# Attention: the weighted values of every second unit in two halves of 256 queries, and the products of a pair of units in another order

## The chip, the cores and the metric

The kernel runs on one core of a Trainium2 chip. The metric is the device time of one execution in microseconds (us): the median of 3 runs before the change is 1863.93 us (1863.89 to 1864.54). Beside it stands one profiled execution, from which all rows of the profile come; its own time is 1863.55 us.

A core has five engines that work side by side, each with its own queue of instructions in a fixed order: PE (matrix products; the loads of its weights are shown apart, as PEld), DVE (elementwise work and reductions), ACT (activations), POOL and SP (here the issuer of DMAs). They wait for one another by semaphores. PE writes its products to PSUM, which has eight banks of 128 partitions by 512 fp32 values.

## The reference

One transformer block over 2048 rows of 512 values: attention with 32 heads of 16, and then a gated mixer.

```python
h = x + _A_ref(_layernorm(x), A_wqkv, A_wo)
...
qkv = (x @ wqkv).reshape(B, S, 3, H, Dh) ...
scores = jnp.einsum("bhqd,bhkd->bhqk", q, k) * scale
p = _softmax(scores, axis=-1)
o = jnp.einsum("bhqk,bhkd->bhqd", p, v)
return o.transpose(...).reshape(B, S, D) @ wo
...
h2 = h + _B_ref(_layernorm(h), ...)
```

The change lies in the attention, in the scores, their maxima and the weighted values; the mixer behind it is the same code in both kernels.

## The kernel before

**Stages.** A first stage normalizes x and makes q, k and v (up to about 172 us of the span). Then comes the attention loop (to about 1408 us), then the mixer.

**The attention loop.** The 32 heads are taken in 8 groups of 4 (`hg`), the 2048 queries in 4 blocks of 512 (`qb`), the keys in 16 blocks of 128 (`kb`). One `(hg, qb, kb)` is a unit, 512 in all. The loop (L744) takes two units a pass, which is called a pair here: unit A with an even `kb`, unit B with `kb1`. PE, ACT, DVE and SP keep the order in which the code is written (`manual_schedule`), so the lines of the loop are the order of their queues.

**A unit's own work.** `score(hg, qb, kb, p)` (L665) is called for p = 0 and 1. It makes two products `s` (L673), for t = 0 and t = 1: keys by queries, 128 by 512. The operands for t = 0 lie in partitions from 0, those for t = 1 in partitions from 64 (`RG` = 64, `KM` = 50 rows). Then ACT takes the exp of both at once into the tile `pt` (L676). The pool of `s` has two buffers of two banks each. `weigh` (L679) makes the weighted values of a unit: for each of the 4 heads a product of 32 columns of weights (the values of the head, a column of ones for the sum, the rest padding) with `pt`, 512 queries wide (L684). The four write to four bands of 32 partitions of the one bank `pv`, and sum over the 16 key blocks there: `start` at `kb == 0`, `stop` at the last. Each fp32 product is two instructions, so a call is eight. `weigh` of a unit runs behind the scores of the next; `prev` is the unit B of the pair before.

**gather.** When a sum of 16 key blocks is finished (at `kb == 0` of the next), `gather` (L687) copies `pv` to SBUF, half by DVE (L690) and half by ACT (L694), and stores it. A `weigh` with `kb == 0` writes the same bank anew. `invert` (at `kb == 6`, L648) takes the reciprocals of the sums, on DVE.

**The maxima.** Softmax needs the maximum of each row of the scores ahead of the exp. `max_pair(m)` (L207) gives eight steps, one product `m` each (L225: 128 queries by 512 keys), which run in the same pair of units as other scores, but `LEAD` = 11 pairs ahead of them. `four[0]` to `four[3]` are `one(1, e, b)`: t = 1, with a DVE maximum over the row (L230). `one(0, 2)` and `one(0, 3)` are the same for t = 0. For the first half of the keys with t = 0 there are `minus`, whose product ACT takes the Abs of (L235), and `plus`, whose product DVE joins with it (L239). The number that a step is called with is its bank, 0 to 2 (`bank`, L202); a step into a bank waits for the DVE or ACT instruction that read it last. There are steps in the pairs with n from 0 to 488, 245 of them; the last eleven pairs have none. In every eighth pair `last` also joins the maxima of a block of queries (`nm`, L245), POOL splits them in two parts (L90, L93), and `max_rows` (L255) transposes them on DVE (L259) and stores them by eight DMAs as rows of `qst`, where a later `score` reads them.

**The order of a pair before.** On PE, with t in brackets and W for the eight instructions of a `weigh`: s(0) s(1) s(0) s(1) of unit A, `four[0]`(1), `one(0,2)`(0), W of `prev`, `minus`(0), [gather], `four[1]`(1), s(0) s(1) of unit B, `four[2]`(1), s(0) s(1), `four[3]`(1), `plus`(0), W of unit A, [`max_rows`], `one(0,3)`(0).

Of the kernel before, what the change touches and what calls it, by code (L numbers as in the profile page):

```python
# [8 lines left out]
F32 = mybir.dt.float32  # L9
# [3 lines left out]
AF = mybir.ActivationFunctionType  # L13
# [5 lines left out]
P = 128  # L19
# [3 lines left out]
DH = 16  # L23
# [3 lines left out]
NB = S // P  # L27
HB = NB // 2
NQ = S // 512
DB = D // P  # L30
HG = H // 4
# [17 lines left out]
def block_kernel(ctx: ExitStack, tc: tile.TileContext, x, wqkv, wo, w_in, w_sp4, b_sp, w_out, out):  # L49
# [154 lines left out]
            return more[i]()  # L204
        return ps_m.tile([P, 512], F32, name=f"m{i}")

    def max_pair(m):  # L207

        g, i = divmod(m, 8)
        hg, qb = divmod(g, NQ)
        q, k, w = qst[g], kst[hg % 2], uvs[hg % 2]
        if i == 0:
            mx[g] = sm.tile([P, 16, 4], F32, name="mx")
            nc.gpsimd.memset(mx[g][:, :8, 3:], LOW)
        c, p = slice(i % 4 * P, i % 4 * P + P), i // 4
        at = lambda t, e: mx[g][:, t * 8 + i, e:e + 1]  # L220

        def scores(t, keys, b):
            r = slice(RG * t, RG * t + KS)
            acc = bank(b)
            nc.tensor.matmul(acc, q[r, p, c], keys[r, p], start=True, stop=True)  # L225
            return acc

        def one(t, e, b):
            acc = scores(t, k[:, :, 512 * e:512 * e + 512], b)
            nc.vector.reduce_max(at(t, e if t else e - 1), acc, axis=AX.X)  # L230

        def minus(b):
            acc = scores(0, w[:, :, 512:], b)
            ab[0] = sm.tile([P, 512], F32, name="ab")
            nc.scalar.activation(ab[0], acc, AF.Abs)  # L235

        def plus(b):
            acc = scores(0, w[:, :, :512], b)
            nc.vector.tensor_tensor_reduce(ab[0], acc, ab[0], 0.5, LOW, ALU.add, ALU.max, at(0, 0))  # L239

        def last(b):
            one(0, 3, b)
            if i == 7:
                nm = sm.tile([P, 2, 8], F32, name="nm")
                nc.vector.tensor_reduce(nm.rearrange("p t i -> p (t i)"), mx.pop(g), axis=AX.X,  # L245
                                        op=ALU.max, negate=True)
                parts = sm.tile([P, 2, 2, 8], F32R, name="mparts")
                split(parts[:, :, 0], parts[:, :, 1], nm, "pool", "pool")
                turned[0] = (g, parts)

        ab = {}
        four = [lambda b, e=e: one(1, e, b) for e in range(4)]
        return [four[0], lambda b: one(0, 2, b), minus, four[1], four[2], four[3], plus, last]

    def max_rows():  # L255

# [398 lines left out]
    with ExitStack() as at:  # L655
# [6 lines left out]
        ps_s = at.enter_context(tc.tile_pool(name="ps_s", bufs=2, space=PSUM))  # L662
        pv = {}

        def score(hg, qb, kb, p):  # L665

            q, k = qst[hg * NQ + qb], kst[hg % 2]
            turn[0] += len(later)
            pool = later[0] if later and turn[0] % 3 == 2 else ps_s
            s = pool.tile([P, 2, 512], F32, name="s")  # L670
            for t in range(2):
                r = slice(RG * t, RG * t + KM)
                nc.tensor.matmul(s[:, t, :], k[r, p, kb * P:(kb + 1) * P], q[r, p, :],  # L673
                                 start=True, stop=True)
            t = pp.tile([P, 2, 512], F32, name="pt")
            nc.scalar.activation(t, s, AF.Exp, scale=DH ** -0.5)  # L676
            return t

        def weigh(hg, qb, kb, pts):  # L679
            if kb == 0:  # L680
                pv[0] = ps_v.tile([P, 512], F32, name="pv")
            for j in range(4):
                c = (4 * kb + j) * VW
                nc.tensor.matmul(pv[0][32 * j:32 * j + 32, :], vst[hg % 2][:, c:c + 32],  # L684
                                 pts[j % 2][:, j // 2, :], start=kb == 0, stop=kb == NB - 1)

        def gather(hg, qb, pool=sm):  # L687

            o = pp.tile([P, 512], F32, name="o", bufs=1)
            nc.vector.tensor_copy(o[:, :256], pv[0][:, :256])  # L690
            if pool is sm and later:
                nc.vector.tensor_copy(o[:, 256:], pv[0][:, 256:])
            else:
                nc.scalar.activation(o[:, 256:], pv[0][:, 256:], AF.Copy)  # L694
            cols = slice(qb * 512, (qb + 1) * 512)
            sums = pool.tile([P, 16], F32, name="sums")
            for j in range(4):
                h = head(hg, j % 2, j // 2)
                nc.sync.dma_start(o_scr[h * DH:(h + 1) * DH, cols], o[32 * j:32 * j + DH, :])
                nc.sync.dma_start(sums[32 * j:32 * j + 32, :], o[32 * j + DH:32 * j + VW, :])  # L700
            sums_[0] = (hg, cols, sums, pool)
# [18 lines left out]
        def more_h(k):  # L720

            for _ in range(k):
                if not pieces:
                    sb = h_rows[len(hns)]
                    acc = later[0].tile([P, 512], F32, name="h")
                    pieces.extend([sb, acc, h_products(sb, acc)])
                sb, acc, products = pieces
                next(products)
                made[0] += 1
                if made[0] % (3 * DB):  # L730
                    continue
                pieces.clear()
                add_h(sb, acc)
                split_o(h_rows[len(hns) + 1], *("pool", "pool") if hns else [None])
                mv, rs = scale_h(sb)
                hns[sb] = e2.tile([P, D], F32, name="hn", bufs=3)
                nc.vector.tensor_scalar(hns[sb], xrs.pop(sb), mv[:, 0:1], rs,
                                        op0=ALU.subtract, op1=ALU.mult)
# [4 lines left out]
        with tc.manual_schedule(engines={E.PE, E.Activation, E.DVE, E.SP}):  # L743
            for n in range(0, len(units), 2):  # L744
                (hg, qb, kb), (_, _, kb1) = units[n:n + 2]
                if hg + 1 < HG and n % 64 < 24 and n % 4 == 0:
                    load_k(hg + 1, [n % 64 // 4])
                if hg + 1 < HG and n % 64 < 12 and n % 4 == 2:
                    load_uv(hg + 1, [n % 64 // 4])
                if hg + 1 < HG and n % 64 == 30:  # L750
                    load_v(hg + 1)
                if kb == 2 and n // NB + 3 < HG * NQ:
                    load_q(n // NB + 3)
                steps = max_pair(m) if m < 8 * HG * NQ else []
                m += 1
                if not steps and not later:
                    maxima.close()
                    later.append(attn.enter_context(
                        tc.tile_pool(name="ps_l", bufs=1, space=PSUM, side="right")))
                step = lambda b: steps and steps.pop(0)(b)  # L760
                pts = [score(hg, qb, kb, 0), score(hg, qb, kb, 1)]
                step(2)
                step(0)
                if prev is None:

                    pv[0] = ps_v.tile([P, 512], F32, name="pv")
                    for j in range(4):
                        nc.tensor.matmul(pv[0][32 * j:32 * j + 32, :], vst[0][:, :32],
                                         vst[0][:, :512], start=True, stop=True)
                else:  # L770
                    weigh(*prev)
                step(1)
                if kb == 0 and n:
                    gather(*units[n - 1][:2])
                step(2)
                pts1 = [score(hg, qb, kb1, 0)]
                step(0)
                pts1.append(score(hg, qb, kb1, 1))
                step(1)
                step(2)  # L780
                if n >= 490:
                    more_h(2 + (n < 494))
                weigh(hg, qb, kb, pts)
                if turned:
                    max_rows()
                step(1)
                prev = (hg, qb, kb1, pts1)
                if kb == 6 and n > NB:
                    invert()
                if n % 32 == 16 and n < 6 * 32:  # L790
                    load_weights(n // 32)
                if n in (476, 482, 492, 504):
                    load_o(h_rows[(476, 482, 492, 504).index(n)])
                if n == 482:
                    split_o(h_rows[0], "pool", "pool")
            weigh(*prev)
            gather(*prev[:2], e2)
# [186 lines left out]
    with ExitStack() as fin:  # L984
# [332 lines left out]
```

## Time and profile before

| | |
|---|---|
| median of 3 runs | 1863.93 us |
| the profiled execution | 1863.55 us |
| its span, first to last instruction | 1861.7 us |
| busy: PE, PEld | 1852.8 us, 1047.3 us |
| busy: DVE, ACT, POOL | 1530.4 us, 1317.8 us, 225.7 us |
| granted clock of PE | 1.00 |

How to read the rows below. A row of the costliest groups or of the groups of a stretch gives line, engine, operation, the tiles written and read, the shapes and the count; then the busy time in us and the mean duration of one in ns; then the idle time of the engine just before them, with what ended it. A row of the timeline gives start and duration in us, engine, line, operation and tiles, the count of instructions merged into the row, and in brackets the idle time before it and its releaser. Products are pipelined: a row's duration reaches from the start to a modelled end, so the start of one product and the start of the next say more than the duration. A row of the stretches gives the window, its length, and then the busy time and count of PE, PEld, DVE, ACT and POOL, the granted clock, the share of the DMA engines and GB/s.

### The profile page before, as it was taken

To read this page: it belongs to the slowest core of one execution; us is meant where nothing else is said; L and a number is where in the kernel's file an instruction comes from. 1 tells how busy PE (TensorE), PEld (TensorE's weight loads), DVE (VectorE), ACT (ScalarE), POOL (GpSimd) and SP (SyncE) were. 2 spreads that over 40 slices of the span, in tenths; PEclk is the share of its full clock that TensorE was granted. 3 is DMA by queue.
4 is the path that set the end of the run, shared out by engine and by line. 5 is a ranking of instruction groups with operands and counts; after the bars stand their busy time and mean duration, and the time that the engine had idled before them with its cause. 6 is when DMAs were issued, how large, how long until landed. Compare 5 with 4: busy or idle time off the path is not lost.

```text
span 1861.7 us, 31964 instructions
## 1 busy us (share of the span) xinstructions
PE 1852.8 (100%) x11410; PEld 1047.3 (56%) x11410; DVE 1530.4 (82%) x3060; ACT 1317.8 (71%) x1696; POOL 225.7 (12%) x305
## 2 busy tenths in 40 slices
PE   9999999999999999999999999999999999999999
PEld 6775444444444444444444444444437889999998
DVE  6487999999999999999999999999935766877664
ACT  3224888888888888888888888888895444434221
POOL 2241000011010100000000000000001756001111
PEclk9999999999999999999999999999999999999999
DMA  6688111221120121022011112100123555768662
GB/s 192 193 191 197 41 24 30 48 53 28 39 57 15 49 44 25 13 51 40 13 39 32 23 29 50 25 14 13 30 56 108 175 160 166 226 186 264 212 191 94
DMA packets 148743, 159.90 MB, mean 86 GB/s; under 512 B 63096, under 2 KB 93320, under 8 KB 147240
## 3 DMA queue, kind: packets, MB, share of 16 engines
q1 hardware_dynamic: 143800, 146.44, 29.7%
q10 hardware_dynamic: 4752, 11.41, 1.6%
q8 instruction: 90, 1.47, 0.3%
q14 instruction: 69, 0.57, 0.1%
q0 software_dynamic: 32, 0.01, 0.0%
HBM read 101.26 MB, written 55.61 MB: 84 GB/s over the span
## 4 chain that ended last, share of the span: by engine, by line
PE 98%; DVE 1%; issue 0%; ACT 0%; DMA 0%; SPq 0%; POOL 0%; POOLq 0%; DVEq 0%; ACTq 0%
PE pv L684 27%; PE m L225 26%; PE s L673 13%; PE acc L96 5%; PE acc L98 5%; PE acc L97 5%; PE g L98 4%; PE g L97 4%; PE g L96 4%; PE acc L617 2%; PE tp L1189 1%; PE h L617 0%; PE tp L885 0%; PE acc L1210 0%; PE tp L369 0%
## 5 line engine op out<-in xcount | busy, mean ns | idle before, releaser
L676 ACT ACTIVATE pt<-s 128x1024 f32<-128x1024 f32 x1024 | 994.1, 1030 | 141.6 <-PE s L673 139.2
L230 DVE TENSOR_REDUCE mx<-m 128x1 f32<-128x512 f32 x1508 | 956.6, 684 | 99.7 <-PE m L225 56.6
L225 PE MATMUL m<-kst,qst 48*128 48x512 f32 x1508 | 605.1, 447 | 0.0
L684 PE MATMUL pv<-pt,vst 128*32 128x512 f32 x4096 | 545.8, 605 | 0.0
L673 PE MATMUL s<-qst,kst 50*128 50x512 f32 x2048 | 465.1, 428 | 0.0
L225 PEld LDWEIGHTS m<-kst,qst 48*128 48x128 f32 x1508 | 262.7, 184 | 316.2 <-DVE mx L230 221.4
L673 PEld LDWEIGHTS s<-qst,kst 50*128 50x128 f32 x2048 | 222.6, 185 | 53.9 <-ACT pt L676 29.8
L225 PE MATMUL m<-uvs,qst 48*128 48x512 f32 x497 | 246.5, 496 | 0.0
L225 PEld LDWEIGHTS m<-uvs,qst 48*128 48x128 f32 x497 | 90.8, 183 | 205.4 <-DVE mx L230 204.6
L684 PEld LDWEIGHTS pv<-pt,vst 128*32 128x32 f32 x4096 | 80.8, 108 | 158.2 <-issue 155.5
L239 DVE CUSTOM_DVE_ANT_0 ab<-m,ab 128x512 f32<-128x512 f32 x249 | 169.6, 681 | 0.0
L235 ACT ACTIVATE ab<-m 128x512 f32<-128x512 f32 x248 | 149.3, 602 | 4.1 <-PE m L225 4.0
L90 POOL CAST mparts<-nm 128x16 fp32r<-128x16 f32 x32 | 6.3, 197 | 880.2 <-DVE nm L245 880.2
L825 ACT ACTIVATE ws<-a 128x512 fp32r<-128x512 f32 x80 | 45.8, 621 | 50.0 <-PE g L98 23.6
L904 ACT ACTIVATE z<-acc 128x464 f32<-128x464 f32 (+2 forms) x64 | 27.6, 456 | 65.3 <-PE acc L98 63.3
L96 PE MATMUL acc<-wi,hT 128*128 128x464 f32 (+2 forms) x196 | 72.8, 371 | 0.0
L98 PE MATMUL acc<-wi,hT 128*128 128x464 f32 (+2 forms) x196 | 71.8, 366 | 0.0
L97 PE MATMUL acc<-wi,hT 128*128 128x464 f32 (+2 forms) x196 | 71.6, 365 | 0.0
L826 DVE TENSOR_TENSOR ws<-a,ws 128x512 fp32r<-128x512 f32 x80 | 56.1, 745 | 13.1 <-ACT ws L825 13.0
L96 PE MATMUL g<-b,ws 128*128 128x344 f32 x192 | 62.6, 326 | 0.0
L88 ACT ACTIVATE part<-acc 128x512 fp32r<-128x512 f32 x32 | 19.1, 598 | 60.8 <-PE acc L98 56.0
L98 PE MATMUL g<-t,ws 128*128 128x344 f32 x192 | 61.3, 319 | 0.0
(200 smaller groups left out, 2121.2 us busy)
## 6 DMA issues: line engine op xcount, KB each, us to landing
a<-in_w_sp SPq DMA_DIRECT2D x80, 256.0 KB
qst<-q_scr SPq DMA_DIRECT2D x192, 64.0 KB
z_scr<-z ACTq DMA_DIRECT2D x32, 344.0 KB
kst<-k_scr SPq DMA_DIRECT2D x42, 256.0 KB
k_scr<-part SPq DMA_DIRECT2D x16, 512.0 KB
q_scr<-part SPq DMA_DIRECT2D x16, 512.0 KB
z<-z_scr SPq DMA_DIRECT2D x14, 344.0 KB
b<-z_scr SPq DMA_DIRECT2D x24, 172.0 KB
```

The costliest lines, as they stand in the source:

```text
L96: nc.tensor.matmul(ps, lh, rh, start=first, stop=False)
L97: nc.tensor.matmul(ps, lh, rl, start=False, stop=False)
L98: nc.tensor.matmul(ps, ll, rh, start=False, stop=last)
L225: nc.tensor.matmul(acc, q[r, p, c], keys[r, p], start=True, stop=True)
L230: nc.vector.reduce_max(at(t, e if t else e - 1), acc, axis=AX.X)
L235: nc.scalar.activation(ab[0], acc, AF.Abs)
L239: nc.vector.tensor_tensor_reduce(ab[0], acc, ab[0], 0.5, LOW, ALU.add, ALU.max, at(0, 0))
L673: nc.tensor.matmul(s[:, t, :], k[r, p, kb * P:(kb + 1) * P], q[r, p, :], start=True, stop=True)
L676: nc.scalar.activation(t, s, AF.Exp, scale=DH ** -0.5)
L684: nc.tensor.matmul(pv[0][32 * j:32 * j + 32, :], vst[hg % 2][:, c:c + 32], pts[j % 2][:, j // 2, :], start=kb == 0, stop=kb == NB - 1)
L825: nc.scalar.activation(hi, src, AF.Copy)
L826: (nc.gpsimd if el == "pool" else nc.vector).tensor_sub(lo, src, hi.bitcast(F32))
```

## The change

In a pair with steps for the maxima, the order on PE becomes: `minus`(0), s(0) s(1) of unit A, `four[0]`(1), s(0), the first half (queries 0 to 255) of `weigh` of `prev`, `one(0,2)`(0), s(1), `one(0,3)`(0), `four[1]`(1), s(0) s(1) of unit B, the second half (queries 256 to 511) of `weigh` of `prev`, [gather], s(0), `four[2]`(1), `plus`(0), s(1), the whole `weigh` of unit A, `four[3]`(1) as `last`, [`max_rows`]. To allow this, `score` is split in two calls (`scores_of`): the product for t = 0, and the product for t = 1 with the exp. `max_pair` gets a second order of steps with `late`, in which `one(1, 3)` is the last. `weigh` takes the columns it is to do. `gather` comes behind the second half, and `max_rows` behind `last`. The pairs without steps, and the first stage's use of `max_pair`, keep their order.

```diff
-    def max_pair(m):
+    def max_pair(m, late=False):
...
-        def last(b):
-            one(0, 3, b)
+        def last(b, *which):
+            one(*which, b)
...
-        return [four[0], lambda b: one(0, 2, b), minus, four[1], four[2], four[3], plus, last]
+        two = lambda b: one(0, 2, b)
+        if late:
+            return [minus, four[0], two, lambda b: one(0, 3, b), four[1], four[2], plus,
+                    lambda b: last(b, 1, 3)]
+        return [four[0], two, minus, four[1], four[2], four[3], plus, lambda b: last(b, 0, 3)]
...
-        def score(hg, qb, kb, p):
+        def score(*unit):
+            first, second = scores_of(*unit)
+            first()
+            return second()
+
+        def scores_of(hg, qb, kb, p):
...
-            for t in range(2):
+            def product(t):
                 r = slice(RG * t, RG * t + KM)
                 nc.tensor.matmul(s[:, t, :], k[r, p, kb * P:(kb + 1) * P], q[r, p, :],
                                  start=True, stop=True)
-            t = pp.tile([P, 2, 512], F32, name="pt")
-            nc.scalar.activation(t, s, AF.Exp, scale=DH ** -0.5)
-            return t
-
-        def weigh(hg, qb, kb, pts):
+            def second():
+                product(1)
+                t = pp.tile([P, 2, 512], F32, name="pt")
+                nc.scalar.activation(t, s, AF.Exp, scale=DH ** -0.5)
+                return t
+
+            return lambda: product(0), second
+
+        def weigh(hg, qb, kb, pts, cols=slice(0, 512)):
...
-                nc.tensor.matmul(pv[0][32 * j:32 * j + 32, :], vst[hg % 2][:, c:c + 32],
-                                 pts[j % 2][:, j // 2, :], start=kb == 0, stop=kb == NB - 1)
+                nc.tensor.matmul(pv[0][32 * j:32 * j + 32, cols], vst[hg % 2][:, c:c + 32],
+                                 pts[j % 2][:, j // 2, cols], start=kb == 0,
+                                 stop=kb == NB - 1 and cols.stop == 512)
...
-                step = lambda b: steps and steps.pop(0)(b)
-                pts = [score(hg, qb, kb, 0), score(hg, qb, kb, 1)]
-                step(2)
-                step(0)
...
+                if steps:
+                    step = lambda b: steps.pop(0)(b)
+                    step(2)
+                    pts = [score(hg, qb, kb, 0)]
+                    step(1)
+                    first, second = scores_of(hg, qb, kb, 1)
+                    first()
...
+                        weigh(*prev, slice(0, 256))
+                    step(0)
+                    pts.append(second())
+                    step(1)
+                    step(2)
+                    pts1 = [score(hg, qb, kb1, 0)]
+                    if prev is not None:
+                        weigh(*prev, slice(256, 512))
+                    if kb == 0 and n:
+                        gather(*units[n - 1][:2])
+                    first, second = scores_of(hg, qb, kb1, 1)
+                    first()
+                    step(0)
+                    step(1)
+                    pts1.append(second())
+                    weigh(hg, qb, kb, pts)
+                    step(0)
+                    if turned:
+                        max_rows()
                 else:
+                    pts = [score(hg, qb, kb, 0), score(hg, qb, kb, 1)]
                     weigh(*prev)
-                step(1)
-                if kb == 0 and n:
-                    gather(*units[n - 1][:2])
-                step(2)
-                pts1 = [score(hg, qb, kb1, 0)]
-                step(0)
-                pts1.append(score(hg, qb, kb1, 1))
-                step(1)
-                step(2)
...
-                weigh(hg, qb, kb, pts)
-                if turned:
-                    max_rows()
-                step(1)
...
```

More of the change, by code (lines that the diff above doesn't have):

```diff
@@ L753, in block_kernel @@
                     load_q(n // NB + 3)
-                steps = max_pair(m) if m < 8 * HG * NQ else []
+                steps = max_pair(m, True) if m < 8 * HG * NQ else []
                 m += 1
@@ L759, in block_kernel @@
                         tc.tile_pool(name="ps_l", bufs=1, space=PSUM, side="right")))
-                step = lambda b: steps and steps.pop(0)(b)
-                pts = [score(hg, qb, kb, 0), score(hg, qb, kb, 1)]
-                step(2)
-                step(0)
[L764 to L769, printed above, removed]
+                if steps:
[5 more added lines that the diff above has]
+                    first()
+                    if prev is None:
+                        pv[0] = ps_v.tile([P, 512], F32, name="pv")
+                        for j in range(4):
+                            nc.tensor.matmul(pv[0][32 * j:32 * j + 32, :], vst[0][:, :32],
+                                             vst[0][:, :512], start=True, stop=True)
+                    else:
+                        weigh(*prev, slice(0, 256))
[17 more added lines that the diff above has]
+                        max_rows()
@@ L770, in block_kernel @@
                 else:
+                    pts = [score(hg, qb, kb, 0), score(hg, qb, kb, 1)]
                     weigh(*prev)
-                step(1)
-                if kb == 0 and n:
-                    gather(*units[n - 1][:2])
-                step(2)
-                pts1 = [score(hg, qb, kb1, 0)]
-                step(0)
-                pts1.append(score(hg, qb, kb1, 1))
-                step(1)
-                step(2)
-                if n >= 490:
-                    more_h(2 + (n < 494))
@@ L783, in block_kernel @@
-                weigh(hg, qb, kb, pts)
-                if turned:
-                    max_rows()
-                step(1)
+                    if kb == 0:
+                        gather(*units[n - 1][:2])
+                    pts1 = [score(hg, qb, kb1, 0), score(hg, qb, kb1, 1)]
+                    if n >= 490:
+                        more_h(2 + (n < 494))
+                    weigh(hg, qb, kb, pts)
+                    if turned:
+                        max_rows()
                 prev = (hg, qb, kb1, pts1)
```

## The prediction

> **What bounds the kernel now.** I read the page first, then the stretches, then the timeline of single pairs. From the page and from the stretch of the attention loop:
>
> ```profile
> span 1861.7 us, 31964 instructions
> PE 98%; DVE 1%; issue 0%; ACT 0%; DMA 0%; SPq 0%; POOL 0%; POOLq 0%; DVEq 0%; ACTq 0%
> L676 ACT ACTIVATE pt<-s 128x1024 f32<-128x1024 f32 x1024 | 994.1, 1030 | 141.6 <-PE s L673 139.2
> L230 DVE TENSOR_REDUCE mx<-m 128x1 f32<-128x512 f32 x1508 | 956.6, 684 | 99.7 <-PE m L225 56.6
> L684 PE MATMUL pv<-pt,vst 128*32 128x512 f32 x4096 | 545.8, 605 | 0.0
> 171.60:1362.00 1190.40, 1190.40 (x7817) 491.11 (x7816) 1094.30 (x2074) 1051.90 (x1252) 50.42 (x112) 1.00 0.16 34
> ```
>
> The chain of waits gives PE 98%, but the stretch (columns: length, then busy time of PE, PEld, DVE, ACT, POOL, then granted clock 1.00) shows DVE at 1094 and ACT at 1052 of 1190 us. So PE leads by less than a tenth, and a reordering can turn either of the others into the bound. The order of a single pair of units (one pass of the loop) is in the timeline:
>
> ```profile
> 900.45 1.06 PE L684 MATMUL pv<-pt,vst 128*32 128x512 f32 x8
> 901.08 1.02 ACT L676 ACTIVATE pt<-s 128x1024 f32<-128x1024 f32 x1
> 901.45 0.50 PE L225 MATMUL m<-uvs,qst 48*128 48x512 f32 x1
> 901.45 0.50 PE L225 MATMUL m<-kst,qst 48*128 48x512 f32 x1
> 901.99 0.60 ACT L235 ACTIVATE ab<-m 128x512 f32<-128x512 f32 x1
> 902.01 1.89 DVE L230 TENSOR_REDUCE mx<-m 128x1 f32<-128x512 f32 x3 [0.27 <-PE m L225]
> 902.15 0.19 PEld L673 LDWEIGHTS s<-qst,kst 50*128 50x128 f32 x2 [0.17 <-ACT pt L676]
> 902.47 1.95 ACT L676 ACTIVATE pt<-s 128x1024 f32<-128x1024 f32 x2
> 902.64 0.18 PEld L225 LDWEIGHTS m<-kst,qst 48*128 48x128 f32 x1 [0.30 <-ACT ab L235]
> 902.76 0.49 PE L225 MATMUL m<-uvs,qst 48*128 48x512 f32 x1
> 903.18 1.06 PE L684 MATMUL pv<-pt,vst 128*32 128x512 f32 x8
> 903.63 0.61 PE L684 MATMUL pv<-pt,vst 128*32 128x512 f32 x4
> 904.18 0.50 PE L225 MATMUL m<-kst,qst 48*128 48x512 f32 x1
> 904.51 0.62 PE L673 MATMUL s<-qst,kst 50*128 50x512 f32 x3
> 904.98 0.40 PE L225 MATMUL m<-kst,qst 48*128 48x512 f32 x1
> 905.02 1.02 ACT L676 ACTIVATE pt<-s 128x1024 f32<-128x1024 f32 x1 [0.59 <-PE s L673]
> 905.30 0.64 PE L684 MATMUL pv<-pt,vst 128*32 128x512 f32 x4
> ```
>
> A block of weighted values (eight `pv` rows, in two passes of four) holds PE alone: 900.45 to 901.45 and 903.18 to 904.18, 1.00 us each. Between the blocks stand the products of scores (`s`) and of the maxima (`m`). Two of them run side by side where one reads partitions from 0 and the other from 64 (both at 901.45); those of one half follow each other. The seven of 904.18 to 905.30 have four in the lower half, and the last of these starts 0.80 after the first: 1.12 us for four steps. A step more or less is about 0.23 (904.51 to 904.98 is two), so I take 0.90 for three steps and 0.67 for two. The other stretch, 901.45 to 903.18, needs five steps but takes 1.73, since it waits for the Abs (0.30) and an exp (0.17). One pair: 900.45 to 905.30, 4.85 us.
>
> Once in eight pairs smaller work comes in:
>
> ```profile
> 700.59 0.22 DVE L245 TENSOR_REDUCE nm<-mx 128x16 f32<-128x64 f32 x1
> 700.72 0.68 DVE L230 TENSOR_REDUCE mx<-m 128x1 f32<-128x512 f32 x1
> 704.42 0.21 DVE L259 STREAM_TRANSPOSE mturned<-mparts 128x32 f32<-128x32 f32 x1
> 739.58 0.22 DVE L245 TENSOR_REDUCE nm<-mx 128x16 f32<-128x64 f32 x1
> 754.00 0.64 PE L684 MATMUL pv<-pt,vst 128*32 128x512 f32 x4
> 759.00 0.16 PEld L684 LDWEIGHTS pv<-pt,vst 128*32 128x32 f32 x8 [0.37 <-issue]
> 1363.68 0.22 DVE L245 TENSOR_REDUCE nm<-mx 128x16 f32<-128x64 f32 x1
> 1364.24 0.22 POOL L93 TENSOR_TENSOR mparts<-nm,mparts 128x16 fp32r<-128x16 f32 x1
> 1364.49 0.21 DVE L259 STREAM_TRANSPOSE mturned<-mparts 128x32 f32<-128x32 f32 x1 [0.60 <-POOL mparts L93]
> ...
> L690 DVE COPY o<-pv 128x256 f32<-128x256 f32 x30 | 12.4, 415 | 0.0
> L694 ACT ACTIVATE o<-pv 128x256 f32<-128x256 f32 x30 | 12.1, 402 | 0.0
> L648 DVE RECIPROCAL rcp<-sums 128x16 f32<-128x16 f32 x30 | 7.3, 243 | 0.0
> L245 DVE TENSOR_REDUCE nm<-mx 128x16 f32<-128x64 f32 x30 | 6.6, 220 | 1.0
> ```
>
> Eight pairs take 700.59 to 739.58, 38.99 us, hardly more than eight times 4.85: this work is nearly hidden today. A pair with a gather is 754.00 to 759.00, 5.00, so 0.15 over the plain one.
>
> **The half blocks.** Per pair one block of 1.00 becomes two of 256 columns, `h1` and `h2`: eight more instructions, of half the columns. No row has a 256-column product of this kind. The two passes of a whole block start 0.45 apart (903.18, 903.63); if all of that went with the columns, a half would take 1.00 - 0.45 = 0.55; if nothing did, 1.00. A part of the 0.45 is the first load of weights, so I take 0.57, near the lower end because the streaming of columns is what the pass does. The Trainium skill (TensorE: Matmul & The Clock Gate, the table of cycles under the matmul cost) gives 262 cycles for 256 columns and 518 for 512, which makes two half passes of 0.23 and a block of 0.55 as an estimate; the sum below would then be 5 us lower, and no run here shows the half yet.
>
> **PE's own sum.** The new order has three groups in place of two. Steps by halves: after the whole block `last`, `minus`, s, s, `four[0]`, s: three; after h1 `two`, s, `one(0,3)`, `four[1]`, s, s: three; after h2 s, `four[2]`, `plus`, s: two. Without waits: 1.00 + 0.90 + 0.57 + 0.90 + 0.57 + 0.67 = 4.61 us. So the better pairing of halves (eight steps for nine) pays for the third block and 0.24 more, if nothing waits.
>
> **What waits instead.** `minus` now opens the pair, so ACT does the Abs before the first exp, and the second group hangs on both ACT and DVE.
> Over ACT, from one whole block's start to the next: block 1.00; `minus` to Abs 0.61 (904.51 to 905.02 is 0.51 for a product whose weights were loaded ahead, and 0.50 against 0.40 long is 0.1 more where they were not); Abs to exp 0.48 (901.99, 902.47); exp to the s that reuses its buffer 1.07 (901.08, 902.15); that s to h2 0.42 (902.76, 903.18); h2 0.57; third group 0.67. Sum 4.82.
> Over DVE: block 1.00; `last` to its reduce 0.56 (901.45, 902.01); reduce to reduce 0.60 (1.89 for three, 0.68 the last); reduce of `four[0]` to the product that reuses its bank 0.68 + 0.05 (what 901.08 + 1.02 to 902.15 shows for a release); two steps 0.67; h2 0.57; 0.67. Sum 4.80.
> I take 4.83 for a plain pair. The 0.24 of PE are thus eaten by two waits in the second group, and the pair is the same as today within some hundredths: 245 pairs (n from 0 to 488) x -0.02 = -5 us. What the hundredths of seven terms leave open is 0.06 a pair, 15 us.
>
> **The transpose of the maxima moves.** Before, `max_rows` stood ahead of `last`, so what `last` left was turned a pair later (700.59, then 704.42), in DVE's idle time. Now it stands behind `last`: DVE reaches the transpose right after `nm`, and must wait for POOL's two conversions of it. The last one of the old loop, where DVE had no other work, shows that length: 1363.68 to 1364.49, 0.81, and 0.21 for the transpose itself: 1.0 us. Queued behind it on DVE is the reduce of `four[0]`; PE's `one(0,3)` waits for that bank, and all of PE behind it. The DVE sum has 0.03 of slack to the plain pair, so it costs nearly whole: 30 x 1.0 = 30 us. Its eight DMA issues on SP go along, a pair earlier, well ahead of the scores that read them. Bounds: 0 if the cover is there after all, 1.1 with some queueing.
>
> **The gather moves behind h2.** Its ACT copy now stands behind three exps, and the next whole block (it starts a new sum in the one `pv` bank) waits for it. Block 1.00, group 0.90, h1 0.57, s to exp 0.61, two exps of 0.91 (1.95 for two, 1.03 the last), copy 0.40, release 0.05: 5.35, against 4.83. So the gather costs 0.52 where it cost 0.15: 30 x 0.37 = 11 us (bounds 0 and 0.5 a gather).
> **The reciprocal** stays at the end of its pair but now lies between `last` and `four[0]`, with 0.03 of slack: 0.2 of its 0.243, 30 x 0.2 = 6 us (bounds 0 and 7).
>
> **Sum.** -5 + 30 + 11 + 6 = +42 us on the profiled execution's own 1863.55 (its span is 1861.7, 1.85 around it): 1905.6, near enough the median 1863.93 to be read as 1906. Parts before and behind the loop, and the eleven pairs without maxima, do the same work as before.
>
> **Rivals.**
> 1. The other side, faster: the two waits in the second group are not met, because the consumers start sooner after a product than I add up, and PE's 4.61 sets the pair. Then 245 x -0.24 = -59; with 0.2 of slack at each of the three stalls they cost 30 x (0.8 + 0.17 + 0) = 29 in place of 47: -59 + 29 = -30, so 1834. For it: PE leads the chain today with 98%. Against: DVE and ACT are at 92% and 88% in the stretch, and the terms are all read from starts. It decides once the plain pair is below 4.85 - 47 / 245 = 4.66.
> 2. The transpose does not stop DVE's chain (POOL done sooner, or `four[0]`'s product late anyway): 1906 - 30 = 1876. Against: POOL's rows are the same work.
> 3. A half block costs a whole one's 1.00, from columns not being what a pass pays for: 0.43 more on the chain, 245 x 0.43 = 105: 2011. For it: the rows of 512 do not separate fixed from streamed time. Against: a pass of 0.45 behind a load of under 0.16 for eight.
> The Trainium skill (TensorEngine Tiling (Array Packing), Key Properties) says that a change of tiling mode, not of the tile, drains TensorE; by it each of the three blocks pays a drain where two did. Rows agree as far as 904.98 to 905.30, 0.32, is more than the step of 0.23. Were that free, h2's side would lose about 0.1 a pair, 24 us.
>
> **How the numbers follow.** The forecast as it stands 0.53, with 1885 to 1930 as its own range from the 15 us of the pair and some of the stalls. Rival 2 0.19; rival 1 0.14; rival 3 0.06; the middle ground where gains and stalls cancel 0.05; the rest beyond 1942 0.03. The likeliest is 1906. The range leaves out most of rival 1 and rival 3: 1860 to 1942. A difference of 0.2%, 3.7 us, is what a measurement of this kernel can tell from none: faster 0.14, same 0.05, slower 0.81.
>
> **What would show it.** In the changed profile: half blocks of 0.57 (start of the first half's `pv` to the next product); a plain pair of 4.83, with PEld waiting ahead of the second group for a reduce and an exp; a DVE row of the transpose with an idle of about 0.6 ahead of it, released by POOL, thirty times; a pair with a gather of 5.35, whose block waits for the ACT copy; eight pairs of 40.4. A plain pair below 4.66, or a transpose without its idle, would make the prediction wrong.

## The result and the profile after

The changed kernel takes 1912.08 us (median of 4 runs, 1911.9 to 1913.42) against 1863.91 for the one before: a ratio of 1.0259 with a 95% interval of 1.0242 to 1.0277, 48.2 us slower. 1906 was predicted. The span of the profiled execution is 1910.1 us. From its page, with the rows that answer to those of before:

```profile
span 1910.1 us, 36059 instructions
PE 89%; DVE 7%; ACT 1%; issue 1%; POOL 1%; DMA 1%; DVEq 0%; POOLq 0%; ACTq 0%
L230 DVE TENSOR_REDUCE mx<-m 128x1 f32<-128x512 f32 x1508 | 955.3, 682 | 127.6 <-PE m L225 100.1
L692 ACT ACTIVATE pt<-s 128x1024 f32<-128x1024 f32 x1024 | 1019.8, 1022 | 35.9 <-PE s L686 26.9
L235 ACT ACTIVATE ab<-m 128x512 f32<-128x512 f32 x248 | 148.1, 597 | 99.2 <-PE m L225 99.2
```

PE still leads the chain that ended last, but with 89% where it had 98%: DVE now holds 7% of it. ACT's idle time has only changed its place: 141.6 us ahead of the exps before, now 99.2 ahead of the Abs, which opens the pair, and 35.9 ahead of the exps. So the waits are not gone, they are elsewhere.

A plain pair, from the timeline of PE, with three rows of the weight loads, two of which name what they waited for:

```profile
905.22 0.64 PE L703 MATMUL pv<-pt,vst 128*32 128x256 f32 x8
905.78 0.50 PE L225 MATMUL m<-kst,qst 48*128 48x512 f32 x1
906.19 0.19 PEld L225 LDWEIGHTS m<-kst,qst 48*128 48x128 f32 x2 [0.23 <-DVE mx L230]
906.45 0.19 PEld L686 LDWEIGHTS s<-qst,kst 50*128 50x128 f32 x2
906.88 0.64 PE L703 MATMUL pv<-pt,vst 128*32 128x256 f32 x8
907.49 0.18 PEld L686 LDWEIGHTS s<-qst,kst 50*128 50x128 f32 x1 [0.46 <-ACT pt L692]
907.49 0.50 PE L686 MATMUL s<-qst,kst 50*128 50x512 f32 x1
908.16 1.06 PE L703 MATMUL pv<-pt,vst 128*32 128x512 f32 x8
909.16 0.49 PE L225 MATMUL m<-kst,qst 48*128 48x512 f32 x1
910.05 0.64 PE L703 MATMUL pv<-pt,vst 128*32 128x256 f32 x8
910.62 0.50 PE L225 MATMUL m<-kst,qst 48*128 48x512 f32 x1
```

From first half block to first half block it is 905.22 to 910.05, 4.83 to 4.84 us, where it was 4.85. A half block takes 0.57 (910.05 to 910.62). The first and third groups run without a hole (909.16 to 910.05 is 0.89, 907.49 to 908.16 is 0.67); the second takes 1.10 (905.78 to 906.88) in place of 0.90. It is held by a reduce at 906.19; the two loads at 906.45 wait for an exp too, which ends at 906.40, but one step of 0.23 behind 906.19 would be 906.42, so that this adds 0.03 at most. And the product behind the second half block comes 0.04 late, at 907.49 instead of 907.45, when an exp frees its buffer. (A bracket counts from the end of PEld's last load, here 907.03, so that it is longer than the wait.)

The pair in which the maxima of a block of queries are joined:

```profile
721.38 0.60 ACT L235 ACTIVATE ab<-m 128x512 f32<-128x512 f32 x1 [0.35 <-PE m L225]
722.07 0.22 DVE L245 TENSOR_REDUCE nm<-mx 128x16 f32<-128x64 f32 x1
722.63 0.22 POOL L93 TENSOR_TENSOR mparts<-nm,mparts 128x16 fp32r<-128x16 f32 x1
722.89 0.21 DVE L263 STREAM_TRANSPOSE mturned<-mparts 128x32 f32<-128x32 f32 x1 [0.60 <-POOL mparts L93]
723.73 0.50 PE L225 MATMUL m<-kst,qst 48*128 48x512 f32 x2 [0.94 <-DVE mx L230]
727.19 0.60 ACT L235 ACTIVATE ab<-m 128x512 f32<-128x512 f32 x1 [0.36 <-PE m L225]
```

Abs to Abs it is 5.81 us, 0.97 over the plain pair. DVE stands still for 0.60 until POOL has split the numbers, and PE for 0.94 behind DVE's reduce.

A pair with a gather:

```profile
694.67 1.06 PE L703 MATMUL pv<-pt,vst 128*32 128x512 f32 x8
698.23 0.64 PE L703 MATMUL pv<-pt,vst 128*32 128x256 f32 x8
699.48 0.41 DVE L710 COPY o<-pv 128x256 f32<-128x256 f32 x1
699.92 0.38 ACT L714 ACTIVATE o<-pv 128x256 f32<-128x256 f32 x1 [0.22 <-DVE o L710]
700.36 1.07 PE L703 MATMUL pv<-pt,vst 128*32 128x512 f32 x8 [0.77 <-ACT o L714]
```

Whole block to whole block it is 5.69 (694.67 to 700.36). The block waits 0.77 for ACT's copy, and that one 0.22 for DVE's.

Eight pairs hold 40.59 us (mean of 28 times eight, from the starts of the Abs): five plain ones of 4.84, one of 4.88 with the reciprocal, 5.81 and 5.70. Before, the same mean was 39.01. The difference, 1.58, times 245 / 8 is 48.4 us: the whole result.

### The profile page after: what moved, and what is told of

It reads as the page before. It is cut to its first block, busy times and chain, and to the rows that moved or that the text cites. A ratio compares the mean times of both kernels' runs of the same rounds, so it can differ in the third digit from the quotient of the medians.

```text
span 1910.1 us, 36059 instructions
## 1 busy us (share of the span) xinstructions
PE 1847.3 (97%) x13362; PEld 1008.9 (53%) x13362; DVE 1534.2 (80%) x3060; ACT 1368.9 (72%) x1696; POOL 226.0 (12%) x305
## 4 chain that ended last, share of the span: by engine, by line
PE 89%; DVE 7%; ACT 1%; issue 1%; POOL 1%; DMA 1%; DVEq 0%; POOLq 0%; ACTq 0%
PE pv L703 27%; PE m L225 20%; PE s L686 12%; PE acc L96 5%; PE acc L98 5%; PE acc L97 5%; DVE mx L230 5%; PE g L98 3%; PE g L97 3%; PE g L96 3%; PE acc L621 2%; ACT o L714 1%; DVE o L710 1%; PE tp L1226 0%; PE h L621 0%
## 5 line engine op out<-in xcount | busy, mean ns | idle before, releaser
L692 ACT ACTIVATE pt<-s 128x1024 f32<-128x1024 f32 x1024 | 1019.8, 1022 | 35.9 <-PE s L686 26.9
L703 PE MATMUL pv<-pt,vst 128*32 128x256 f32 (+1 forms) x6048 | 597.7, 467 | 24.0 <-ACT o L714 24.0
L225 PE MATMUL m<-kst,qst 48*128 48x512 f32 x1508 | 578.5, 479 | 28.8 <-DVE mx L230 28.3
L686 PE MATMUL s<-qst,kst 50*128 50x512 f32 x2048 | 573.7, 423 | 0.7 <-ACT pt L692 0.7
L225 PEld LDWEIGHTS m<-kst,qst 48*128 48x128 f32 x1508 | 230.1, 183 | 410.0 <-DVE mx L230 354.8
L686 PEld LDWEIGHTS s<-qst,kst 50*128 50x128 f32 x2048 | 275.0, 185 | 140.7 <-ACT pt L692 96.9
L703 PEld LDWEIGHTS pv<-pt,vst 128*32 128x32 f32 x6048 | 119.3, 108 | 268.8 <-issue 241.4
L225 PE MATMUL m<-uvs,qst 48*128 48x512 f32 x497 | 221.4, 446 | 0.0
L235 ACT ACTIVATE ab<-m 128x512 f32<-128x512 f32 x248 | 148.1, 597 | 99.2 <-PE m L225 99.2
```

The source lines that it names most:

```text
L703: nc.tensor.matmul(pv[0][32 * j:32 * j + 32, cols], vst[hg % 2][:, c:c + 32], pts[j % 2][:, j // 2, cols], start=kb == 0, stop=kb == NB - ...
```

## The experiments

All times are medians of 4 to 10 runs; the kernel before ran beside them on the same chip, with medians of 1864.1 to 1864.2 us.

| run | median us | ratio to before [95%] | eight pairs, us |
|---|---|---|---|
| changed kernel | 1912.08 | 1.0259 [1.0242, 1.0277] | 40.59 |
| e1_rows_back | 1888.02 | 1.0128 [1.0113, 1.0143] | 39.80 |
| e2_old_order_at_gather | 1929.56 | 1.0346 [1.0328, 1.0363] | 41.17 |
| e3_both | 1904.32 | 1.0213 [1.0198, 1.0228] | 40.33 |
| e4_two_tiles | 1916.55 | 1.0276 [1.0261, 1.0291] | 40.58 |
| e5_split_alone | 1865.12 | 1.0003 [0.9994, 1.0013] | 39.06 |
| e6_order_alone | 2027.68 | 1.0872 [1.0855, 1.0889] | 44.32 |
| e7_short_reduce | 1884.21 | 1.0105 [1.0089, 1.0121] | 39.67 |
| e8_short_reduce_exp | 1828.26 | 0.9805 [0.9788, 0.9823] | 37.88 |
| e9_banks | 1872.17 | 1.0042 [1.0027, 1.0057] | 39.27 |
| e10_copy_early | 1877.71 | 1.0073 [1.0058, 1.0088] | 39.45 |
| e11_short_abs | 1883.30 | 1.0105 [1.0088, 1.0122] | 39.65 |

### e1: the transpose a pair later

```diff
                     weigh(hg, qb, kb, pts)
-                    step(0)
                     if turned:
                         max_rows()
+                    step(0)
```

> The changed kernel with one line moved: max_rows stands ahead of the last step again, so the maxima are transposed a pair later. Theory (DVE stood still behind POOL's conversions, and PE behind DVE): the pair with the join of the maxima falls from 5.81 us to at most 4.95, 30 times, and the median from 1912 by 26 to 29 us to 1883 to 1886. Rival (that pair would wait for another engine at the same place): less than 10 us off, 1902 or more.

24 us came back, a little less than the 26 to 29. From this run's timeline:

```profile
710.84 0.60 ACT L235 ACTIVATE ab<-m 128x512 f32<-128x512 f32 x1 [0.35 <-PE m L225]
711.53 0.22 DVE L245 TENSOR_REDUCE nm<-mx 128x16 f32<-128x64 f32 x1
711.67 3.24 DVE L230 TENSOR_REDUCE mx<-m 128x1 f32<-128x512 f32 x5
715.43 0.21 DVE L263 STREAM_TRANSPOSE mturned<-mparts 128x32 f32<-128x32 f32 x1
715.88 0.60 ACT L235 ACTIVATE ab<-m 128x512 f32<-128x512 f32 x1 [0.36 <-PE m L225]
```

The idle ahead of the transpose is gone: it now stands 3.9 us behind `nm`, with POOL long done. The pair is 5.04 here, though, and not 4.84. `nm` still lies between the last reduce and that of `four[0]`: from the start of the one to the end of the other it is 1.54 us (710.81 to 712.35), where a plain pair has 1.29. That leaves 0.2 of the 0.97 as the price of `nm` itself, which the old order hid, and puts the result just outside what was expected. The rival falls.

### e2 and e3: the old order in the gather's pairs

```diff
-                steps = max_pair(m, True) if m < 8 * HG * NQ else []
+                steps = max_pair(m, kb > 0) if m < 8 * HG * NQ else []
...
-                if steps:
+                if steps and kb == 0:
...
+                    pts = [score(hg, qb, kb, 0), score(hg, qb, kb, 1)]
+                    step(2)
+                    step(0)
...
+                        weigh(*prev)
+                    step(1)
+                    if n:
+                        gather(*units[n - 1][:2])
...
+                elif steps:
```

> The changed kernel, but in the pairs with kb == 0 (one in eight) the old order: a whole block for the unit before, the gather behind it, the scores of unit A first. Theory (the gather behind the second half makes the next block wait for the copies of the bank): these pairs fall from 5.69 us to 5.0 to 5.1, and the median by 18 to 21 us to 1891 to 1894. Rival (the copies cost the same wherever they stand, as work for ACT and DVE): 1905 or more.

> Both of the above together. Theory (two separate prices, and a plain pair that is worth as much as before): the sum of both, 1912 - 29 - 20 = 1863, within 3 us of the kernel before. Rival (the plain pair's new order has a price of its own that the stalls cover): 1870 or more; rival (it has a gain of its own): 1858 or less.

Both missed. e2 is 17 us slower than the changed kernel, not 20 faster, and e3 is 16 slower than e1. From the starts of the Abs in e3, the gather's pair and its two neighbours together take 15.9 us (7.50 + 3.11 + 5.30) where three plain pairs take 14.5. The timeline of e3 shows where, in the pair behind the gather's:

```profile
656.15 0.68 DVE L239 CUSTOM_DVE_ANT_0 ab<-m,ab 128x512 f32<-128x512 f32 x1
656.89 0.18 PEld L225 LDWEIGHTS m<-uvs,qst 48*128 48x128 f32 x1 [0.20 <-DVE mx L239]
657.04 0.69 DVE L230 TENSOR_REDUCE mx<-m 128x1 f32<-128x512 f32 x1 [0.20 <-PE m L225]
657.79 0.18 PEld L225 LDWEIGHTS m<-kst,qst 48*128 48x128 f32 x1 [0.60 <-DVE mx L230]
```

`minus` (656.89) goes to bank 2, which the old order's `plus` has just filled and DVE read until 656.83. `four[0]` (657.79) goes to bank 1, which the old order's last step filled, and whose reduce ends at 657.73. Each order gives banks so that the step next to use one comes late; where one follows the other that is no longer so. By their times alone e2 and e3 would fit their rivals (the copies cost the same anywhere; the new order has a price of its own), but the plain pairs of e3 are 4.84 long like those of the changed kernel. e9 takes the seam away.

### e9: the same with the banks named anew

Against e3:

```diff
-                    step(2)
-                    step(0)
+                    step(1)
+                    step(2)
...
                         weigh(*prev)
-                    step(1)
+                    step(0)
...
```

> As e3_both, but in the pairs of the old order the banks of the steps are named anew (2 to 1, 0 to 2, 1 to 0), so that the step next to use a bank is not the one that has just filled it. Theory (in e3_both the pair behind a gather waits for banks: its minus for plus, its four[0] for the last reduce, and that ate the gain): a gather's pair and its two neighbours together fall from 15.93 us to about 15.0, and the median from 1904 by 27 us to 1877. Rival (a change between the two orders costs by itself, by exps that come late): 1895 or more.

1872.2: 32 us less than e3, more than the 27 expected. The three pairs hold 14.8 us (6.92 + 3.04 + 4.86), so a gather costs 0.3 in place of the 0.85 of the changed kernel. The reading of e3 stands, and with it that of the gather: the same two copies cost at most 0.3 here, and ACT's starts without a wait in each of the thirty. So it was the gather's place, and not its work, that made most of the 0.85. Of the kernels with the new order that do the whole computation it is the fastest, and still slower than the one before.

### e10: the copy ahead, by DVE alone

```diff
-            nc.vector.tensor_copy(o[:, :256], pv[0][:, :256])
-            if pool is sm and later:
-                nc.vector.tensor_copy(o[:, 256:], pv[0][:, 256:])
+            if pool is sm:
+                nc.vector.tensor_copy(o, pv[0])
             else:
+                nc.vector.tensor_copy(o[:, :256], pv[0][:, :256])
                 nc.scalar.activation(o[:, 256:], pv[0][:, 256:], AF.Copy)
...
-                    step(2)
+                    step(2, *([held] if kb == 0 and n else []))
...
                         gather(*units[n - 1][:2])
+                        held.pop()()
```

`held` keeps the reduce of `four[1]` until behind the gather; its product stays where it is.

> As e1_rows_back, and in the gather's pair DVE alone copies the whole bank, ahead of the reduce of four[1], whose product stays where it is. Theory (the next whole block waits for ACT's copy, which stands behind three exps and DVE's copy): the block starts 0.5 to 0.7 us earlier, DVE's reduces come 0.6 later and eat about half of that, the pair falls from 5.69 by 0.2 to 0.4, and the median from 1888 by 6 to 12 us to 1876 to 1882. Rival (the copies' work is what costs): 1886 or more.

```profile
679.60 1.07 PE L707 MATMUL pv<-pt,vst 128*32 128x512 f32 x8
683.87 0.69 DVE L715 COPY o<-pv 128x512 f32<-128x512 f32 x1
684.61 1.07 PE L707 MATMUL pv<-pt,vst 128*32 128x512 f32 x8
```

The block follows the copy's end (684.56) at once; 5.01 from block to block. The pair by its Abs is 5.21, more than the expected 0.2 to 0.4 below 5.69, but the next is 4.97, 0.13 over the plain one, for the reduces that came later; together they gain 0.35. The median is 10 us below e1, in the expected 6 to 12.

### e4: two tiles for the gather

```diff
-            o = pp.tile([P, 512], F32, name="o", bufs=1)
-            nc.vector.tensor_copy(o[:, :256], pv[0][:, :256])
+            o = [pp.tile([P, 256], F32, name=f"o{i}", bufs=1) for i in range(2)]
+            nc.vector.tensor_copy(o[0], pv[0][:, :256])
...
-                nc.scalar.activation(o[:, 256:], pv[0][:, 256:], AF.Copy)
+                nc.scalar.activation(o[1], pv[0][:, 256:], AF.Copy)
...
```

> The changed kernel, but the two copies of a gather write to two tiles in place of one. Theory (ACT's copy waits for DVE's because both read the one bank pv, whose readers are kept apart): nothing changes, 1912 within 3 us, and ACT's copy still shows an idle of about 0.2 us ahead of it, ended by DVE. Rival (it waits because both write the one tile o): the copy starts 0.3 us earlier, the pair falls from 5.69 to about 5.36, and the median by 10 us to 1902.

```profile
699.97 0.38 ACT L714 ACTIVATE o<-pv 128x256 f32<-128x256 f32 x1 [0.22 <-DVE o L710]
```

The wait is the same, and so are the eight pairs (40.58). So it is not the common tile; the one thing that the two copies still share is the bank. The Trainium skill (PSUM — Partial Sum Buffer, PSUM bank collisions raise a hardware error) says that two engines must not touch one bank in the same partitions at once, two reads included, and that accesses of this kind have to be put in order; this trace agrees, with 0.22 us of waiting thirty times. The time missed the expected 1912 within 3 us: the kernel lost 4 us as a whole, and they lie behind the attention loop. The edit also makes sixteen stores of the eight that a gather had. The last reciprocal waits 2.53 us for them and starts at 1471.43, where it started at 1469.11; PE then stands still for 2.50 ahead of the products of `o` at 1480.98, which the changed kernel does not, and the granted clock from 1480 to 1500 is 0.91 in place of 1.00.

### e5: the two halves behind each other

```diff
+                elif steps:
+                    weigh(*prev, slice(0, 256))
+                    weigh(*prev, slice(256, 512))
                 else:
                     weigh(*prev)
```

In the order of before. 

> The kernel before with one edit: the first block of a pair is made in two halves of 256 queries right behind each other, nothing between them. As many instructions as in the changed kernel. Theory (a half costs its columns, and what makes 2 x 0.57 of 1.00 is filling and draining at the change between kinds of products, which is missing here): the two halves together take 1.00 to 1.05 us, and the median rises by 0 to 12 us to 1864 to 1876. Rival (each half has a fixed price for its eight instructions): 1.14 us, and up to 34 us more, 1890 to 1898.

```profile
901.08 1.07 PE L684 MATMUL pv<-pt,vst 128*32 128x256 f32 x16
902.08 0.50 PE L225 MATMUL m<-uvs,qst 48*128 48x512 f32 x1
```

Sixteen instructions in 1.00 us, as long as eight of 512 columns, and a median that can't be told from that of before. So the split is free; the 2 x 0.57 - 1.00 = 0.14 a pair of the changed kernel comes from standing apart, with other products between the halves. No run tells the change between the kinds of products from the first load of each half. The 0.14 is the bound on what the rule of the Trainium skill quoted in the prediction (TensorEngine Tiling (Array Packing), Key Properties: a change of tiling mode drains) is worth here.

### e6: the new order without the halves

```diff
-                        weigh(*prev, slice(0, 256))
+                        weigh(*prev)
...
-                    if prev is not None:
-                        weigh(*prev, slice(256, 512))
```

> The changed kernel with one edit: the whole block of the unit before stands at the place of the first half, and nothing at that of the second. Two blocks a pair, the new order of the products. Theory (the second group and what hangs on its exps come 0.43 us later, and the whole block of unit A must wait for the second exp): a plain pair of about 5.2 us, 0.38 more than 4.84, and a median of 1912 + 245 x 0.38 = 2005, less 10 to 25 for stalls that are covered. Rival (PE's own sum leads: one block fewer to fill and drain): 4.4 to 4.6 us a pair, 1800 to 1860.

A plain pair takes 5.26, near the 5.2; the rival (PE's own sum, 4.4 to 4.6) falls. The median is 23 us above the 2005, since the stalls were not covered: the pair with the join takes 5.6, the one with a gather 6.1 to 7.4, and the one behind it 5.2 to 6.8. This run also shows a lower granted clock, 0.97 to 0.98 over the loop where the changed kernel has 1.00: it is 1.00 in the plain pairs and in a gather's pair of 6.11 (789.86 to 795.97), but 0.82 in one of 7.26 (745.03 to 752.29) and 0.93 in the pair behind that. All that these pairs take beyond 6.11 and 5.26 comes to 32 us, more than the 23 by which the median is over; what lowers the clock there stays open. So the order needs the halves: the whole block delays the second exp, and all that hangs on it, by the other half.

### e7, e11 and e8: which engine holds the plain pair

```diff
-            nc.vector.reduce_max(at(t, e if t else e - 1), acc, axis=AX.X)
+            nc.vector.reduce_max(at(t, e if t else e - 1), acc[:, :256], axis=AX.X)
```

> The changed kernel, but the maxima of DVE's plain reductions are taken over 256 of the 512 keys of each product; the other half is left out. Theory (a chain over ACT and one over DVE of nearly one length, 4.82 and 4.80 us): with DVE's gone, ACT's holds the plain pair at 4.80 or more, and only the stalls shrink: 1895 to 1912. Rival (DVE alone holds the pair): the pair falls towards PE's own sum of 4.61, and the median by 40 us or more, to 1870 or less.

The plain pair stays at 4.84: DVE does not hold it alone. The stalls shrank more than expected (the join's pair to 5.28, the gather's to 5.35 to 5.45), which brought the median to 1884, below the expected 1895 to 1912.

```diff
-            nc.scalar.activation(ab[0], acc, AF.Abs)
+            nc.scalar.activation(ab[0][:, :256], acc[:, :256], AF.Abs)
-            nc.vector.tensor_tensor_reduce(ab[0], acc, ab[0], 0.5, ...
+            nc.vector.tensor_tensor_reduce(ab[0][:, :256], acc[:, :256], ab[0][:, :256], 0.5, ...
```

> As e7_short_reduce, and the Abs and DVE's join with it take 256 of their 512 keys too; the other half is left out. The exps are whole. Theory A (the plain pair of 4.84 is held over ACT by the Abs ahead of the first exp): the Abs is 0.2 us shorter, and a plain pair falls to 4.62 to 4.66, the median by 40 us or more below e7's 1884. Theory B (a second chain over ACT of nearly the same length: the second exp starts only behind the first half block, and the last scores wait for its buffer; whole block 1.00, group 0.90, half 0.57, product to exp 0.61, exp to its buffer 1.07, third group 0.67, together 4.82): a plain pair of 4.78 to 4.83, and 1870 or more.

The plain pairs take 4.83 to 4.84, so theory B. A plain pair of e11, PE with the exps of ACT:

```profile
915.08 1.07 PE L703 MATMUL pv<-pt,vst 128*32 128x512 f32 x8
916.08 0.50 PE L225 MATMUL m<-kst,qst 48*128 48x512 f32 x1
916.98 0.64 PE L703 MATMUL pv<-pt,vst 128*32 128x256 f32 x8
917.55 0.50 PE L686 MATMUL s<-qst,kst 50*128 50x512 f32 x1
918.18 2.96 ACT L692 ACTIVATE pt<-s 128x1024 f32<-128x1024 f32 x3 [0.23 <-PE m L225]
918.45 0.64 PE L703 MATMUL pv<-pt,vst 128*32 128x256 f32 x8
919.25 0.50 PE L686 MATMUL s<-qst,kst 50*128 50x512 f32 x1 [0.16 <-ACT pt L692]
919.92 1.07 PE L703 MATMUL pv<-pt,vst 128*32 128x512 f32 x8
```

The second group runs without a hole now (917.55 to 918.45, 0.90). But the second product of unit A's second pair of scores stands behind the first half block, at 917.55; its exp starts at 918.18, with ACT idle for 0.23 ahead of it (the bracket names the product `m` that starts beside it), and is done at 919.20; the product at 919.25 needs its buffer. All the time that the shorter Abs and reduces save is waited for there: from 915.08 this chain is 1.00 + 0.90 + 0.57 + 0.63 + 1.07 + 0.67 = 4.84, the whole pair.

e8 was built on e7, with the Abs whole again; that is the run that its expectation calls the one before:

```diff
-                nc.scalar.activation(t, s, AF.Exp, scale=DH ** -0.5)
+                nc.scalar.activation(t[:, 0, :], s[:, 0, :], AF.Exp, scale=DH ** -0.5)
...
-                                 pts[j % 2][:, j // 2, cols], ...
+                                 pts[j % 2][:, 0, cols], ...
```

> As the run before, and the exps are taken for the first of the two 512-wide products only, which the weighted values then use for all four heads; the other exps are left out. PE's instructions are the same. Theory (PE's own sum is 4.61 us a pair, and waits for DVE and ACT made 4.84 of it): a plain pair of 4.58 to 4.66, and a median of 1912 - 245 x 0.22 = 1858, less 20 to 45 for the stalls, so 1813 to 1840. Rival (PE itself needs 4.8 for the three groups and blocks): 4.78 or more a pair, 1860 or more.

```profile
900.62 1.07 PE L703 MATMUL pv<-pt,vst 128*32 128x512 f32 x8
901.61 0.50 PE L225 MATMUL m<-kst,qst 48*128 48x512 f32 x1
902.51 0.64 PE L703 MATMUL pv<-pt,vst 128*32 128x256 f32 x8
903.08 0.50 PE L225 MATMUL m<-kst,qst 48*128 48x512 f32 x1
903.98 0.64 PE L703 MATMUL pv<-pt,vst 128*32 128x256 f32 x8
904.55 0.50 PE L686 MATMUL s<-qst,kst 50*128 50x512 f32 x1
905.22 0.64 PE L703 MATMUL pv<-pt,vst 128*32 128x512 f32 x4
```

Block 0.99, group 0.90, half 0.57, group 0.90, half 0.57, group 0.67: 4.60 us, term by term the sum that was written down for PE without waits. With the same instructions on PE, the time fell to 1828 us. So the 0.24 between 4.60 and 4.84 is waiting for ACT and DVE, and no work of PE.

## Why the prediction was right

**The half block** was put at 0.57 and took 0.57; the bound of 1.00 (rival 3) is out, and e5 shows that the eight extra instructions have no price of their own: two halves take 1.00 next to each other.

**PE's own sum**, 4.61, is confirmed by e8 with 4.60. Rival 1 needed it to set the pair; the pair is 4.84, so it falls.

**The plain pair** was put at 4.83 and is 4.84. The size was right, and both waits that were named show up in the second group, for the reduce (906.19) and for the exp (906.45). But neither of the two chains given for it is what holds the pair alone. The prediction named Abs, first exp, and the product that reuses that exp's buffer (4.82), and a chain over DVE (4.80). e7 and e11 shorten them, and the pair does not move. What holds it then is a third chain, which the prediction did not list: whole block, first group, half block, second exp, and the product of unit B that waits for that buffer. Its terms are rows of before too: 1.00 + 0.90 + 0.57 + 0.61 + 1.07 + 0.67 = 4.82. In the unshortened kernel all three lie within 0.02 of each other, by these sums; the DVE chain shows its wait at 906.19, the third one at 907.49. That the chain left out is no longer than the two listed is luck: with a longer one the forecast for the plain pair would have been too low.

**The transpose** was put at 1.0 a time and cost 0.97; the stall has the place and the releaser that were named (0.60 behind POOL's conversions). The 1.0 starts with `nm` (1363.68), so it holds that reduce too, which the prediction put down to the transpose's move with the rest. e1 parts them: moving the transpose back gives 24 us of the 29, and the 0.2 a time that stay are `nm`, which had a cover in the old order only. Rival 2 falls.

**The gather** is the term that was mis-sized: 5.35 was predicted, 5.69 measured, 30 x 0.34 = 10 us. The step "its ACT copy now stands behind three exps" left out that the copy also waits for DVE's copy of the same bank, which stands behind three reduces. The row of before with 0.40 for ACT's copy had shown no wait, because DVE's was long over there.

**The reciprocal** was put at 0.2 and cost 0.04 (4.88 against 4.84), 30 x 0.16 = 5 us too much. From DVE's timeline of the changed kernel:

```profile
716.47 0.69 DVE L230 TENSOR_REDUCE mx<-m 128x1 f32<-128x512 f32 x1 [0.33 <-PE m L225]
717.07 0.24 DVE L652 RECIPROCAL rcp<-sums 128x16 f32<-128x16 f32 x1
717.23 0.63 DVE L230 TENSOR_REDUCE mx<-m 128x1 f32<-128x512 f32 x1
```

It starts 0.09 before the reduce ahead of it is over, and the reduce behind it ends 1.39 after the start of the first, 0.10 later than the 1.29 of a plain pair. `nm`, of nearly the same length, reads what that reduce writes and starts 0.03 behind its end; there it is 1.54, or 0.25 later (e1). With the transpose as well it is 2.33, 1.04 later. The pairs grew by 0.04, 0.19 and 0.97, each 0.06 to 0.07 less than the delay. So the DVE chain has that much slack, where the prediction took 0.03, and the reciprocal's price was its delay and not its length.

**The sum:** +42 was predicted, +48 measured; 10 more at the gather, 5 less at the reciprocal, 1 less at the transpose, and 2 more in the roundings of the plain pairs. That the first two misses have opposite signs is luck. That no repair (e1, e3, e9, e10) comes below the time before agrees with its first term: the new order itself gains some hundredths of a microsecond a pair, and the small work that the old order hid must be hidden anew.

## What to carry to other kernels

Where three engines lie as near to each other as here (1190, 1094 and 1052 us busy before), a better packing of one of them is worth only what the chains through the others leave: add up every way around the loop that passes a buffer's reuse, each exp and its buffer too, not only those that the old waits name. Small work that costs nothing has a place at which it costs nothing; when the order around it changes, look again at where it stands in its queue, at what it waits for, and at which engine read the same bank just ahead of it. Two orders of steps that share a rotation of banks can't be joined without looking at the seam: e3 lost 32 us to names of banks alone.

## What had not been expected of the hardware

Two half blocks next to each other cost exactly a whole one (1.00 us, sixteen instructions against eight), while the same two apart cost 0.57 each. The two copies of one bank by ACT and DVE run one after the other (0.22 us of waiting, with one tile or with two). At one place in DVE's queue an instruction of 0.24 us that does not read the result of the reduce ahead delayed the next reduce by 0.10 us, and one of 0.22 us that does read it by 0.25.
